# Second weight gather, two memsets and the first angle table rearranged in a spectral layer with a gated FFN

## The chip, the cores and the metric

The kernel runs on one core of a Trainium2 chip. The metric is device time in microseconds of one execution. Five engines work from queues of their own, in order: PE (matrix multiply), DVE (vector), ACT (scalar, activations), POOL (GpSimd) and SP (issues DMAs). They wait for each other through semaphores.

## The reference

The reference is a layer in two halves: a two-dimensional Fourier filter over the normalised input, added to the input, and a gated feed-forward block over the normalised result.

```python
def _A_ref(x, w_r, w_i):          # x: 1 x 2048 x 576
    X = rfft2(x.astype(float32), axes=(-2, -1))
    X = X * (w_r + 1j * w_i)      # 2048 x 289
    return irfft2(X, s=(S, D), axes=(-2, -1)).astype(bfloat16)

def _B_ref(x, w_gate, w_up, w_down):   # 576 -> 4608 -> 576
    return (gelu(x @ w_gate) * (x @ w_up)) @ w_down

h  = x + _A_ref(layernorm(x), w_r, w_i)
h2 = h + _B_ref(layernorm(h), w_gate, w_up, w_down)
```

## The kernel before, in words

The 2048 rows are held as 128 partitions by 16 rows (`h` from 0 to 15, 576 wide). The length-2048 transform is split as 16 x 128. The order of work is written out by hand: each engine runs its instructions in the order in which the program issues them, and nothing reorders them.

**Stage 1, row transforms.** For each row `h`, statistics are taken (on DVE with `sd`, L364, or on ACT with `ln_act`, L121), POOL turns them into 1/sigma (`ln_rstd`, L131: an add L133 and a power L134, four rows at a time), DVE normalises the row (L137, writes `xn`), and PE multiplies it by a 16-point table (`row16` L319, `rests` L335). ACT copies the products from PSUM to `Bt` (`evict` L346, `evict4` L352; the last `evict4`, of rows 12 to 15, is DVE's). `fill` (L309) issues matmuls whose results nobody uses, ahead of rows 0 and 8.

**Tables.** Beside this, three tables are made. `F16` is the 16-point table. `DT` (with `DF`, a part of it in other partitions) is the 576-point column table: sines on ACT (L393), mirrored by DVE (`mirror`, L404), copied into `DF` by L454 and L455; POOL sets `DF` and one column of `DT` to zero first (L446, L447). `TF` holds the twiddle angles' sines and cosines for nine column groups: `first` is the first two of them, `rest` the other seven. For `rest`, DVE makes an integer angle (`angle_a` L237), masks it to 2047 (L264), subtracts 1024 (L265), drops the sign (`angle_c`, L224), and ACT takes `sine` (L271) and `cosine` (L274); L277 makes the negative sine. For `first`, POOL makes the angle in float and takes off whole turns (`first_a` L249, L250; `first_b` L255 to L257), DVE drops a sign (L224), ACT takes the sines (L260, L261). SP then turns `TF` into `TI` by a transposing DMA (`turn_tf`, L280), once for `first`, once for `rest`; thirteen small DMAs (L475) that build `DQ` stand between the two in SP's queue.

**Filter weights.** `WR` and `WI` come half by plain DMA, half by a gather of POOL (`gather`, L382, into `wm_r` and `wm_i`), from which SP copies on (L462). POOL halves two columns of each (L468).

**Stage 2, column loop** (L709). For each column group in `order` (1 to 7, then 0), `f2` (L520) multiplies by the column table for groups k and k+8 and `f2_out` (L531) copies the product out of PSUM as `pq`; `f3` (L537, L538) applies the twiddles, its two halves copied by ACT as `g` and `hs` (L559); `sum_of` (L570) and `wmul` (L588 to L609) on DVE form the filtered spectrum `Zt`; `i3` (L628) starts the inverse with `TI`. For the first group, `f2_out` of group k+8 is DVE's, in two halves, and `sum_of` reads the second half straight from PSUM. PSUM has four buffers of two banks, shared by all these products, so that a product waits for the copy of the one four before it.

**Stage 3.** Inverse columns, residual, and the feed-forward block (L941 and L984), which fills the time from 70 us on with matmuls.

The steps that the change touches are issued in this order before: `gather(0)` after the rstd of rows 4 to 7; `first_a` ahead of the rstd of rows 8 to 11; `first_b` between that and the rstd of rows 12 to 15; behind that on POOL `gather(1)` and the two memsets L446, L447, then the `Zt` memsets (L460). On DVE, the sign drop for `first`, the last `evict4`, `angle_a(rest)`, the negative sine of `first`, `angle_b(rest)`, the copies L531 of the second column product (group 9), `angle_c(rest)`. On ACT, the `rest` sine and cosine stand between the first `pq` copy and the first `g`.

Of the kernel before, what the change touches and what calls it, by code (L numbers as in the profile page):

```python
# [9 lines left out]
ACT = mybir.ActivationFunctionType  # L10
ALU = mybir.AluOpType
FP32 = mybir.dt.float32
# [8 lines left out]
P = 128  # L21
S = 2048
# [5 lines left out]
JH = JP // 2  # L28
# [8 lines left out]
PI = 3.1415925  # L37
# [5 lines left out]
def kernel_body(  # L43
# [12 lines left out]
    V = nc.vector  # L56
    A = nc.scalar
    G = nc.gpsimd
# [23 lines left out]
    zerob = const("zerob", 0.0)  # L82
    pib = const("pib", PI)
    npib = const("npib", -PI)
    hpib = const("hpib", 0.5 * PI)
# [19 lines left out]
    DT = keep.tile([P, 3, 2, 2, JH], BF16, name="DT")  # L105
    D3 = DT[:, 2]
    DF = keep.tile([P, 2, 2, JH], BF16, name="DF")
# [13 lines left out]
    def ln_act(h):  # L121
        for i, fn, sc in ((0, ACT.Identity, 1.0 / D), (1, ACT.Square, 1.0 / D**0.5)):
            junk = roll.tile([P, D], BF16, name="junk", tag="junk", bufs=2)
            A.activation(junk[:], h_sb[:, h, :], fn, scale=sc, accum_out=mv[:, h, i : i + 1])  # L124
# [6 lines left out]
    def ln_rstd(dst, src, lo, hi):  # L131
        sl = slice(lo, hi)
        G.tensor_scalar(dst[:, sl], src[:, sl, 1], 1e-5, None, op0=ALU.add)  # L133
        G.tensor_tensor(dst[:, sl], dst[:, sl], mhalf[:, sl], ALU.pow)  # L134
# [27 lines left out]
    TF = sp.tile([P, 9, 3, P], BF16, name="TF")  # L162
# [6 lines left out]
    def tmp(name, shape, dtype=I32):  # L169
        return scr.tile(shape, dtype, name=name)  # L170
# [15 lines left out]
    q16 = tmp("q16", [P, P], FP32)  # L186
# [10 lines left out]
    C23 = 8388608.0  # L197
# [17 lines left out]
    s2p = tmp("s2p", [P, 1], FP32)  # L215
# [4 lines left out]
    ks = tmp("ks", [P, 9], FP32)  # L220
    V.tensor_scalar(ks[:], kv[:], s2p[:, 0:1], 0.125, op0=ALU.mult, op1=ALU.mult)

    def drop_sign(dst, src):
        V.tensor_scalar(  # L224
            dst.bitcast(I32),
            src.bitcast(I32),
            1,
            1,
            op0=ALU.logical_shift_left,
            op1=ALU.logical_shift_right,  # L230
        )

    pr, ab = tmp("pr", [P, 9, P]), tmp("ab", [P, 9, P], FP32)

    def angle_a(sl):
        n = sl.stop - sl.start
        V.scalar_tensor_tensor(  # L237
            pr[:, sl],
            q16[:].unsqueeze(1).to_broadcast([P, n, P]),
            s2p[:, 0:1],  # L240
            ks[:, sl].unsqueeze(2).to_broadcast([P, n, P]),
            op0=ALU.mult,
            op1=ALU.add,
        )

    qs, prf, abf = (tmp(n, [P, w, P], FP32) for n, w in (("qs", 1), ("prf", 2), ("abf", 2)))

    def first_a():
        G.tensor_scalar(qs[:, 0], q16[:], s2p[:, 0:1], None, op0=ALU.mult)  # L249
        G.tensor_tensor(  # L250
            prf[:], qs[:].to_broadcast([P, 2, P]), ks[:, 0:2].unsqueeze(2).to_broadcast([P, 2, P]), ALU.add
        )

    def first_b():
        G.tensor_scalar(abf[:], prf[:], 1.0 / S, C23, op0=ALU.mult, op1=ALU.add)  # L255
        G.tensor_scalar(abf[:], abf[:], -C23, -float(S), op0=ALU.add, op1=ALU.mult)
        G.tensor_tensor(prf[:], prf[:], abf[:], ALU.add)  # L257

    def first_sines():
        A.activation(TF[:, 0:2, 2, :], prf[:], ACT.Sin, bias=zerob[:], scale=2.0 * PI / S)  # L260
        A.activation(TF[:, 0:2, 1, :], abf[:], ACT.Sin, bias=hpib[:], scale=-2.0 * PI / S)  # L261

    def angle_b(sl):
        V.tensor_scalar(pr[:, sl], pr[:, sl], 2047, None, op0=ALU.bitwise_and)  # L264
        V.tensor_scalar(ab[:, sl], pr[:, sl], -1024.0, None, op0=ALU.add)  # L265

    def angle_c(sl):
        drop_sign(ab[:, sl], ab[:, sl])

    def sine(sl):  # L270
        A.activation(TF[:, sl, 2, :], pr[:, sl], ACT.Sin, bias=pib[:], scale=-2.0 * PI / S)  # L271

    def cosine(sl):
        A.activation(TF[:, sl, 1, :], ab[:, sl], ACT.Sin, bias=nhpib[:], scale=2.0 * PI / S)  # L274

    def minus_sine(sl):
        V.tensor_scalar(TF[:, sl, 0, :], TF[:, sl, 2, :], -1.0, None, op0=ALU.mult)  # L277
# [12 lines left out]
    def row_table():  # L290
        V.scalar_tensor_tensor(
            F16[:, 0:2, :],
            iu[:].rearrange("p c l -> p (c l)").unsqueeze(1).to_broadcast([P, 2, P]),
            0.0,
            fs[:].unsqueeze(1).to_broadcast([P, 2, P]),
            op0=ALU.is_equal,
            op1=ALU.mult,
        )
# [2 lines left out]
        V.tensor_scalar(F16[:, 2, :], F16[:, 0, :], -1.0, None, op0=ALU.mult)  # L301

    ps_f = {}
    FILL = {0: 14, 8: 12}

    def fill(dst, n):

# [3 lines left out]
    def row16(h):  # L311
        if h % 2 == 0 or h == H - 1:
            ps_f[h] = two("f2t")
        f2t, b = (ps_f[h], 0) if h in ps_f else (ps_f[h - 1], 1)
        fill(f2t[:, b, :], FILL.get(h, 0))
        x = xn[:, h, :]
# [64 lines left out]
    def gather(i):  # L381
        G.indirect_dma_start(  # L382
            out=wm[i][:],
            out_offset=None,
            in_=(A_w_r, A_w_i)[i].rearrange("(a r) j -> a (r j)", r=8),
            in_offset=bass.IndirectOffsetOnAxis(ap=rev[:, 0:1], axis=0),
        )
# [4 lines left out]
    def col_sin(r, src, bias):  # L392
        A.activation(  # L393
            DT[:, :, :, r, 0:JM],
            src[:].rearrange("p t (a j) -> p t a j", a=2),
            ACT.Sin,
            bias=bias[:],
            scale=-2.0 * PI / D,
        )
# [8 lines left out]
    first, rest = slice(0, 2), slice(2, 9)  # L408
    for h in (1, 3, 5, 7, 9, 11):
        ln_act(h)  # L410
    row_table()
    sd(0, 2)
    minus_row()
# [14 lines left out]
    sd(8)  # L428
    norms(4, 8)
    rests(4)  # L430
    first_a()
    sd(10, 12)
    ln_fin(slice(9, 12, 2))
    ln_rstd(rstd, mv, 8, 12)
    col_sin(1, pd, zerob)
    col_sin(0, kd, hpib)
    evict(4, 6)
    evict4(4)
    sd(13, 14, 15)
    flush()  # L440
    first_b()
    norms(8, 12)
    ln_rstd(rstd, mv, 12, 16)
    rests(8)
    gather(1)
    G.memset(DF[:], 0.0)  # L446
    G.memset(DT[:, :, 1, :, JH - 1], 0.0)  # L447
    norms(12, 16)
    rests(12)
    evict(8, 10)  # L450
# [2 lines left out]
    mirror(0)  # L453
    V.tensor_copy(DF[0:32], D3[0:32])  # L454
    V.tensor_copy(DF[96:128], D3[96:128])  # L455
    drop_sign(abf[:], prf[:])
    evict(12, 14, 15)
    evict4(12)
    for z in Zts:
        G.memset(z[:].rearrange("p a w b j -> p (a w b) j")[:, :, JW:], 0.0)  # L460
    for w, t in ((WR, wm[0]), (WI, wm[1])):
        nc.sync.dma_start(w[:, 9 : H + 1, 0:J], t[:].rearrange("p (r j) -> p r j", r=8))  # L462
    first_sines()
    angle_a(rest)
    minus_sine(first)
    turn_tf(first)
    for w in (WR, WI):
# [21 lines left out]
            )  # L489
    G16v = [G16[:, sign].rearrange("p x q -> p (x q)") for sign in range(2)]  # L490
    A.activation(G16v[0], pt[:, 0, 0 : 2 * P], ACT.Copy, scale=G_SCALE)
    angle_b(rest)

    xn_pool.__exit__(None, None, None)
    spw = tc.tile_pool(name="spw", bufs=1)
# [34 lines left out]
    def f2_out(c, copy=A.copy, rs=slice(0, 2)):  # L530
        copy(  # L531
            pq[c][:, rs].rearrange("p r (j a) -> p r j a", a=2),
            pq_ps[c][:, :, 0:JP].rearrange("p a (r j) -> p r j a", r=2)[:, rs],
        )
# [30 lines left out]
    def sum_of(k, half):  # L565
        g, hs = gk[k], hk[k]
        if half == 0:
            xab[k] = wk.tile([P, 2, 2, JP], BF16, name="xab", tag="xab", bufs=2)
        x = xab[k]
        V.tensor_tensor(  # L570
            x[:, 1, ::-1, 0:J] if half else x[:, 0, :, 0:J],
            g[:, :, 0:J],
            hs[:, :, 0:J],
            ALU.add if half else ALU.subtract,
        )
# [132 lines left out]
    n = len(order)  # L708
    for i in range(n + 1):  # L709
        last = i >= n  # L710
        if not last:
            f2(order[i])
            if i != 1:
                f2_out(order[i])
        if i == 0:
            f2(order[0] + 8)
            for r in range(2):
                f2_out(order[0] + 8, V.tensor_copy, slice(r, r + 1))
            angle_c(rest)
            sine(rest)  # L720
            cosine(rest)
            minus_sine(rest)
            V.tensor_scalar(G16v[1], G16v[0], -1.0, None, op0=ALU.mult)

        if 1 <= i <= n:
            f3(order[i - 1], 0)
            f3(order[i - 1], 1)
            if i == 1:
                f2_out(order[1])
                sum_of(order[0], 0)  # L730
                sum_of(order[0], 1)
            else:
                if i == 2:
                    turn_tf(rest)
                    pre = [load_gu(g) for g in range(3)]
                    nc.sync.dma_start(wd_a[:], wd_view[:, 0:NWA, :])
                wmul(order[i - 2], i - 1, order[i - 1])
        if not last and i:
            f2(order[i] + 8)
            f2_out(order[i] + 8)  # L740
        if last:
            inv_cols(0, 0)
            inv_cols(0, 1)
        if i >= 3:
            for s in range(3):
                i3(order[i - 3], s)
        if last:
            wmul(order[i - 1], i)
        if i == 1:
            scr_pool.__exit__(None, None, None)  # L750
            eop = ctx.enter_context(tc.tile_pool(name="eop", bufs=1, side="right"))
            EO = [eop.tile([P, 5, H, 2, 4, 8], BF16, name=f"EO{x}", tag=f"EO{x}") for x in range(2)]
# [209 lines left out]
    for tcnk in range(4):  # L962
        for gi in range(NG):
# [7 lines left out]
            n = tcnk * NG + gi  # L971
# [91 lines left out]
```

## Time and profile before

| what | value |
|---|---|
| median of 3 runs | 499.56 us (499.13 to 500.4) |
| profiled execution | 498.99 us, span of its instructions 497.2 us |
| granted TensorE clock | 1.0 |
| PE busy | 485.7 us (98%) |
| DVE, ACT, POOL busy | 225.4, 159.4, 31.4 us |
| chain that ended last | PE 93%, DVE 2%, POOL 2%, ACT 1%, DMA 1%, issue 1% |

The span runs from the first to the last instruction. A busy time is a union over the whole span; an engine that is busy for a third of it can still be the one that others wait for in a short stretch. The chain is followed back from the last instruction, at each step to what released it. In the timelines a row is: start in us, length in us, engine, line, operation, what is written and read, how many instructions are merged, and in brackets the idle time before it with what ended it.

### The profile page before, as it was taken

How to read it: one execution, taken by the hardware profiler on the slowest of the kernel's cores; microseconds unless marked ns; L12 is line 12 of the kernel's file. 1: busy time of each engine (PE TensorE's matmuls, PEld its weight loads, DVE VectorE, ACT ScalarE, POOL GpSimd, SP SyncE). 2: the span in 40 equal slices, each digit the busy share in tenths (PEclk: the TensorE clock that was granted, in tenths of full speed). 3: DMA queues.
4: the chain of work that ended last, by engine and by line, in shares of the span. 5: the costliest groups of instructions: out<-in, count | busy, mean ns of one | idle time of the engine just before them, and what ended most of it. 6: DMA issues, size and time to landing. Idle time of an engine off the chain costs nothing.

```text
span 497.2 us, 12763 instructions
## 1 busy us (share of the span) xinstructions
PE 485.7 (98%) x5715; PEld 337.4 (68%) x5715; DVE 225.4 (45%) x448; ACT 159.4 (32%) x284; POOL 31.4 (6%) x82
## 2 busy tenths in 40 slices
PE   6889999999999999999999999999999999999997
PEld 3467789885579965555599855555799655555995
DVE  8999884698632157533311244333221333333111
ACT  8789973322311022232300132323110223233000
POOL 7700010011110001100000000000000000000000
PEclk9999999999999999999999999999999999999999
DMA  8539979949991029988730079987700277770000
GB/s 283 158 86 173 246 145 200 207 101 201 212 213 19 3 68 198 202 157 157 153 73 3 1 167 190 197 157 149 146 3 1 78 156 154 158 150 2 13 15 24
DMA packets 89549, 62.33 MB, mean 125 GB/s; under 512 B 23190, under 2 KB 88086, under 8 KB 89494
## 3 DMA queue, kind: packets, MB, share of 16 engines
q1 hardware_dynamic: 89206, 60.34, 60.2%
q0 software_dynamic: 288, 1.18, 0.8%
q8 instruction: 44, 0.72, 0.6%
q14 instruction: 11, 0.09, 0.1%
HBM read 52.65 MB, written 2.36 MB: 111 GB/s over the span
## 4 chain that ended last, share of the span: by engine, by line
PE 93%; DVE 2%; POOL 2%; ACT 1%; issue 1%; DMA 1%; POOLq 0%; DVEq 0%
PE gu L941 56%; PE acc L984 27%; PE cs_ps L679 2%; PE acc L1003 2%; PE eo_ps L628 2%; PE pq_ps L520 2%; PE y_ps L813 1%; ACT junk L124 1%; PE gh_ps L538 1%; POOL rstd L134 1%; PE gh_ps L537 1%; DVE xn L137 1%; DMA h_sb<-in_A_x_dram 1%; POOL wm_r L382 0%; PE eo_ps L652 0%
## 5 line engine op out<-in xcount | busy, mean ns | idle before, releaser
L941 PE MATMUL gu<-Bt,wgu 64*128 64x512 bf16 (+1 forms) x2646 | 270.6, 363 | 0.0
L941 PEld LDWEIGHTS <-wgu 64*128 64x128 bf16 x2646 | 151.7, 94 | 115.4 <-issue 0.3
L950 DVE TENSOR_TENSOR P_sb<-g_sb,gu 128x512 bf16<-128x512 f32 (+1 forms) x156 | 100.2, 644 | 140.4 <-ACT g_sb L949 140.4
L949 ACT ACTIVATE g_sb<-gu 128x512 f32<-128x512 f32 (+1 forms) x156 | 88.0, 564 | 193.5 <-PE gu L941 192.2
L984 PEld LDWEIGHTS <-P_sb 64*128 64x128 bf16 x2160 | 122.3, 94 | 10.8
L984 PE MATMUL acc<-wd,P_sb 64*128 64x288 bf16 x1440 | 90.9, 283 | 0.0
L993 DVE TENSOR_TENSOR part<-part,acc 128x576 f32<-128x576 f32 x15 | 11.3, 754 | 112.6 <-ACT part L992 112.6
L992 ACT COPY part<-acc 128x576 f32<-128x576 f32 x15 | 9.6, 638 | 122.8 <-PE acc L984 122.8
L984 PE MATMUL acc<-wd_a,P_sb 64*128 64x288 bf16 x720 | 46.8, 283 | 0.0
L520 PE MATMUL pq_ps<-DT,Bt 128*128 128x290 bf16 x64 | 12.3, 286 | 0.7 <-ACT g L559 0.7
L941 PE MATMUL gu<-Bt,wgu_e 64*128 64x256 bf16 (+1 forms) x162 | 12.5, 305 | 0.0
L838 DVE TENSOR_SCALAR hrow<-h_sb,mv,rstd 128x1152 bf16<-128x1152 bf16 x14 | 12.1, 867 | 0.5 <-POOL rstd L876 0.5
L995 DVE TENSOR_TENSOR h_sb<-h_sb,part 128x576 bf16<-128x576 bf16 x15 | 11.4, 758 | 0.5
L520 PEld LDWEIGHTS <-Bt 128*128 128x128 bf16 x96 | 9.2, 97 | 3.4 <-issue 0.9
L134 POOL TENSOR_TENSOR rstd<-rstd,mhalf 128x1 f32<-128x1 f32 (+1 forms) x16 | 11.4, 713 | 1.3
L319 PE MATMUL f2t<-F,xn 128*128 128x256 bf16 x64 | 8.1, 273 | 3.2 <-DVE xn L137 3.1
L941 PEld LDWEIGHTS <-wgu_e 64*128 64x128 bf16 x162 | 10.4, 94 | 1.2
L133 POOL TENSOR_SCALAR rstd<-mv 128x1 f32<-128x1 f32 (+1 forms) x16 | 3.8, 237 | 116.3 <-DVE mv L119 116.0
L309 PE MATMUL f2t<-h_sb,ident 128*128 128x512 bf16 x26 | 7.4, 445 | 3.7 <-DMA h_sb<-in_A_x_dram 3.7
L679 PE MATMUL cs_ps<-DQ,EO 58*128 58x290 bf16 x144 | 10.8, 283 | 0.0
L531 ACT CAST pq<-pq_ps 128x580 bf16<-128x580 f32 x15 | 9.8, 664 | 0.2
L319 PEld LDWEIGHTS <-xn 128*128 128x128 bf16 x64 | 5.8, 98 | 5.8 <-DVE xn L137 4.9
(151 smaller groups left out, 283.3 us busy)
## 6 DMA issues: line engine op xcount, KB each, us to landing
wgu<-in_B_w_gate_dram SPq DMA_DIRECT2D x46, 432.0 KB
wgu<-in_B_w_up_dram SPq DMA_DIRECT2D x46, 432.0 KB
wd_a<-in_B_w_down_dram SPq DMA_DIRECT2D x1, 1728.0 KB
wd<-in_B_w_down_dram SPq DMA_DIRECT2D x1, 1728.0 KB
wd<-in_B_w_down_dram SPq DMA_DIRECT2D x6, 288.0 KB
out_dram<-h_sb SPq DMA_DIRECT2D x3, 576.0 KB
h_sb<-in_A_x_dram SPq DMA_DIRECT2D x4, 288.0 KB
h_sb<-in_A_x_dram SPq DMA_DIRECT2D x2, 576.0 KB
```

Source lines behind the costliest of these rows:

```text
L134: G.tensor_tensor(dst[:, sl], dst[:, sl], mhalf[:, sl], ALU.pow)
L319: T.matmul(f2t[:, b, t * 2 * P : (t + 1) * 2 * P], lhsT=x[:, d0 : d0 + P], rhs=F16[:, n : n + 2, :], start=(n == 0), stop=(n == 1),)
L520: T.matmul(ps[:, par, 0:JP], lhsT=Bt[:, t, col], rhs=DT[:, t // 2, par] if t < 4 else DF[:, par], start=(t == par), stop=(t == 4),)
L628: T.matmul(pv[:, n], lhsT=z[:, a, w].rearrange("p b j -> p (b j)"), rhs=TI[:, ts[k], 1 - a : 3 - a, :], start=(a == 0), stop=(a == 1),)
L679: T.matmul(ps[:, e, 0:JP], lhsT=EO[x][rows, w, 2 * g : 2 * g + 2].rearrange("p h e k l -> p (h e k l)"), rhs=DQ[rows, w] if w or e else DT ...
L838: V.tensor_scalar(hrow[:], h_sb[:, h, :].rearrange("p (r k) -> p r k", k=64).unsqueeze(2).to_broadcast([P, NR, 2, 64]), mv2[:, h, 0:1], rs ...
L941: T.matmul(gu[:, c, 0:n], lhsT=w[rows, r, i * P : (i + 1) * P], rhs=hl[tcnk % 2][rows, r, lo:hi], start=(r == 0), stop=(r == NR - 1),)
L949: A.activation(g_sb, gu[:, 0, 0:n], ACT.Gelu_apprx_tanh)
L950: V.tensor_tensor(p_sb(f)[:, lo:hi], g_sb, gu[:, 1, 0:n], ALU.mult)
L984: T.matmul(accs[i][:, c, 0:DH], lhsT=p_sb(f)[rows, st * P : (st + 1) * P], rhs=wd[f // NWA][rows, f % NWA, c * DH : (c + 1) * DH], start=( ...
L993: V.tensor_tensor(part, part, accs[1][:, :, 0:DH], ALU.add)
L995: V.tensor_tensor(hv, hv, part, ALU.add)
```

## The change

`gather(1)` is issued directly behind the rows 4 to 7 products and ahead of the rstd of rows 8 to 11; the memsets of `DF` and of a `DT` column are issued ahead of the row table, before POOL's first rstd work. The first angles are made as integers by two POOL instructions (angle only, one per group, behind the rstd of rows 8 to 11), and masked, shifted and sign-dropped by DVE after the last `evict4`, with ACT's `sine` and `cosine` in place of the two float forms. The late angles (`rest`) all move behind the DVE copies of the second column product: `angle_a` and `angle_b` at once, `sine` behind the second `pq` copy of ACT, and the other steps (now `angle_s` and `angle_c`) behind the first group's `sum_of`, with `cosine` after the following `f2_out`. `fill` ahead of row 0 has 16 matmuls, not 14.

```diff
-    qs, prf, abf = (tmp(n, [P, w, P], FP32) for n, w in (("qs", 1), ("prf", 2), ("abf", 2)))
     def first_a():
-        G.tensor_scalar(qs[:, 0], q16[:], s2p[:, 0:1], None, op0=ALU.mult)
-        G.tensor_tensor(
-            prf[:], qs[:].to_broadcast([P, 2, P]), ks[:, 0:2].unsqueeze(2).to_broadcast([P, 2, P]), ALU.add
-        )
-    def first_b():
-        G.tensor_scalar(abf[:], prf[:], 1.0 / S, C23, op0=ALU.mult, op1=ALU.add)
-        G.tensor_scalar(abf[:], abf[:], -C23, -float(S), op0=ALU.add, op1=ALU.mult)
-        G.tensor_tensor(prf[:], prf[:], abf[:], ALU.add)
-    def first_sines():
-        A.activation(TF[:, 0:2, 2, :], prf[:], ACT.Sin, bias=zerob[:], scale=2.0 * PI / S)
-        A.activation(TF[:, 0:2, 1, :], abf[:], ACT.Sin, bias=hpib[:], scale=-2.0 * PI / S)
+        for k in range(2):
+            G.tensor_scalar(pr[:, k], q16[:], s2p[:, 0:1], ks[:, k : k + 1], op0=ALU.mult, op1=ALU.add)
     def angle_b(sl):
         V.tensor_scalar(pr[:, sl], pr[:, sl], 2047, None, op0=ALU.bitwise_and)
+    def angle_s(sl):
         V.tensor_scalar(ab[:, sl], pr[:, sl], -1024.0, None, op0=ALU.add)
...
-    FILL = {0: 14, 8: 12}
+    FILL = {0: 16, 8: 12}
...
         ln_act(h)
+    G.memset(DF[:], 0.0)
+    G.memset(DT[:, :, 1, :, JH - 1], 0.0)
     row_table()
...
     rests(4)
-    first_a()
+    gather(1)
     sd(10, 12)
     ln_fin(slice(9, 12, 2))
     ln_rstd(rstd, mv, 8, 12)
+    first_a()
...
-    first_b()
     norms(8, 12)
     ln_rstd(rstd, mv, 12, 16)
     rests(8)
-    gather(1)
-    G.memset(DF[:], 0.0)
-    G.memset(DT[:, :, 1, :, JH - 1], 0.0)
     norms(12, 16)
...
-    drop_sign(abf[:], prf[:])
     evict(12, 14, 15)
     evict4(12)
...
-    first_sines()
-    angle_a(rest)
+    angle_b(first)
+    angle_s(first)
+    angle_c(first)
+    sine(first)
+    cosine(first)
     minus_sine(first)
     turn_tf(first)
...
-    angle_b(rest)
...
                 f2_out(order[0] + 8, V.tensor_copy, slice(r, r + 1))
-            angle_c(rest)
-            sine(rest)
-            cosine(rest)
-            minus_sine(rest)
-            V.tensor_scalar(G16v[1], G16v[0], -1.0, None, op0=ALU.mult)
+            angle_a(rest)
+            angle_b(rest)
...
             if i == 1:
                 f2_out(order[1])
+                sine(rest)
                 sum_of(order[0], 0)
                 sum_of(order[0], 1)
+                angle_s(rest)
+                angle_c(rest)
+                minus_sine(rest)
+                V.tensor_scalar(G16v[1], G16v[0], -1.0, None, op0=ALU.mult)
...
             f2_out(order[i] + 8)
+            if i == 1:
+                cosine(rest)
```

## The prediction

> **What bounds the kernel now.** The chain on the page gives PE 93% of the span, and the busy strip shows PE at 9 from the third slice on. Read in order of time, the chain is PE without a break from 31.42 us to the end; only the first 31 us belong to others. The change touches only what is issued before about 36 us, so its worth is how much earlier PE's unbroken run begins, no more. First view: the chain in order of time (start, length, what).
>
> ```profile
> 18.36 1.05 POOL rstd L134
> ...
> 19.43 3.16 DVE xn L137 x4
> 22.59 0.81 DVE DT L404 x4
> ...
> 28.71 1.04 ACT TF L274
> 29.75 0.53 ACT g L559
> 30.28 1.09 ACT pq L531 x2
> ...
> 31.42 0.28 PE gh_ps L538
> ```
>
> Four normalisations take 3.16 us here; the same four take 1.64 us at 11.24. Second view: DVE's timeline, cut to two of the normalisations of rows 8 to 15, and POOL's beside it.
>
> ```profile
> 17.29 0.83 DVE L137 TENSOR_SCALAR xn<-h_sb,mv,rstd 128x576 bf16<-128x576 bf16 x1
> ```
>
> ```profile
> 19.84 2.08 DVE L137 TENSOR_SCALAR xn<-h_sb,mv,rstd 128x576 bf16<-128x576 bf16 x1
> ```
>
> ```profile
> 17.09 0.87 POOL L257 TENSOR_TENSOR prf<-prf,abf 128x256 f32<-128x256 f32 x1
> ...
> 19.58 1.12 POOL L382 DMA_INDIRECT wm_i<-in_A_w_i_dram,rev  x1 [0.18 <-issue]
> 20.71 0.59 POOL L446 MEMSET DF<- 128x580 bf16 x1
> 21.23 0.14 POOL L447 MEMSET DT<- 128x6 bf16 x1
> 21.27 0.48 POOL L460 MEMSET Zt<- 128x120 bf16 x3
> 21.84 0.54 POOL L468 TENSOR_SCALAR WR<-WR 128x34 bf16<-128x34 bf16 x1
> ```
>
> A normalisation alone takes 0.42 us. Row 9's took 0.83 and ended 0.16 after L257 did; row 13's took 2.08 and ended only when the gather and five memsets had passed. That is 1.66 us lost to POOL's train. Third view: ACT's timeline, because ACT must copy out what those rows yield.
>
> ```profile
> 18.83 1.93 ACT L346 CAST Bt<-f2t 128x1024 bf16<-128x1024 f32 x2 [1.39 <-PE f2t L319]
> 20.64 0.60 ACT L352 CAST Bt<-f 128x512 bf16<-128x512 f32 x1
> 22.62 1.99 ACT L346 CAST Bt<-f2t 128x1024 bf16<-128x1024 f32 x3 [1.37 <-PE f2t L319]
> ...
> 28.71 1.04 ACT L274 ACTIVATE TF<-ab,nhpib 128x896 bf16<-128x896 f32 x1 [0.89 <-DVE ab L224]
> ...
> 32.52 0.65 ACT L559 CAST hs<-gh_ps 128x578 bf16<-128x578 f32 x1
> ```
>
> ACT idles 1.37 us for row 13 before 22.62. Its copy hs of the second column pair ends at 33.17; DVE's sum for that pair starts at 33.20 and DVE then works without a gap in rounds of 3.57 us (L588 at 35.43, 39.00, 42.58, 46.15), PE in rounds of 3.56. So **the end of that hs copy sets the pace of the loop**: the forecast is its new time.
>
> **Part 1, POOL's second gather and memsets.** They leave the rows 12 to 15. The gather now stands behind the first, which ends at 12.79: with the idle 0.2 and 1.12 to 1.37 (the two gathers' rows) it ends at 14.1 to 14.4, where POOL stood at 14.13 before. Beside it DVE runs statistics, not normalisations. Its transfer now meets the end of the first WI load and the first gather's (landed at 14.1 and 16.15), and SP can issue the WI copy some 6 us earlier; nobody needs WI before about 31, so a slow landing costs nothing by itself. Then sq, mv, rstd, pow as before (14.13 to 16.04, 1.91): 16.0 to 16.3, needed by DVE at 17.00. Then the two new angle products, 0.4 each by L199's rows (two operations, 128x146, 0.38 to 0.40) or 0.63 by L249's: 16.9 to 17.6. I take 0.45, near L199, which has the same two operations. The last rstd pair (18.05 to 19.40, 1.35) then ends at 18.5 to 19.0, and rows 8 to 11 occupy DVE until about 18.8, so row 12 starts near 18.9 and not 19.43. The Zt memsets (0.48) and the WR product (0.54) still fall beside rows 13 and 14 and may hold DVE up to 1.1 us: all four are done at 20.3 to 21.5. ACT is the later one. Its copies for rows 8 to 15 follow at 0.91, 0.90, 0.51, 0.91, 0.48 and 0.60 (starts in the trace, 18.83 to 21.15 and 22.62 to 24.61): 18.83 + 4.31 = 23.14, not 24.61. **1.47 us gained**, and rows 13 and 15 are in time if done by 20.4 and 21.8.
>
> Here one rule of the Trainium skill speaks against the change. SBUF — State Buffer, section "Who interferes with whom", says that of a GpSimd instruction and a DVE one in a two-port mode the first issued has the shared port pair for its whole length while the other blocks. Row 9 behind L257 agrees (0.83 us); rows 5 to 7 beside the first gather do not (1.30 us for three). By the rule the later angle product, if it ends at 17.6, holds row 8 and moves ACT's start by 0.3 us; the sum would then gain 0.3 and not 0.6.
>
> **Part 2, what is late next.** PE's first column product starts 0.11 after ACT's last copy (24.61 to 24.72); twelve matmuls end 1.66 after that (24.72 to 26.38). DVE's copies of the second product then start at 23.14 + 0.11 + 1.66 + 0.05 = 24.96; at 27.32 before, since the late angles stood ahead of them. Behind these copies DVE now runs: copies 0.74, angle_a 1.17, the mask 0.53, two sums 1.36, minus 1024 0.66, sign drop 0.65 (spacings of L531, L237, L264, L570, L265, L224), 5.11 together. ACT's late cosine can start at 30.07, where it started at 28.71. Behind it in ACT's queue are the third pq copy, g and hs of the second pair: 0.95 + 0.54 + 0.54 + 0.65 = 2.68. The hs copy ends at 32.75, not 33.17: **0.42 us**, the other 1.05 of the 1.47 having gone back to the longer chain through the late angles. DVE reaches its sum at about 31.9 and waits for ACT.
>
> The first angles do not lie on that path: sine and cosine wait for three DVE steps (0.29 each by L224 on 128x256, 0.03 between) behind the last L352 copy, about 22.95, so the cosine ends near 24.4, then G 0.3 and the first pq copy, ended near 25.2; PE needs it with the second product's copy at 25.4. If DVE is held there, it costs one for one beyond 0.2.
>
> **Part 3, SP's queue.** The first table transpose (L280) starts at 26.28, behind L277 on DVE; it can now start near 24.5. Thirteen DQ issues and the second transpose follow without a gap (27.73 to 41.01), so the latter ends 1.8 us earlier. In the round at 43.01 PE's weight load began 0.33 after Zt was written (42.65), against 0.10 and 0.15 in the rounds before: I put the other **0.2 us** down to that transpose, and count it back.
>
> **Parts at nothing.** Two more fill matmuls (0.22 each, L309) go into PE's idle 0.72 before 9.05. DF and DT memsets (0.59, 0.14) at 5.9 stand before a POOL step that waited for ACT until 6.59; the pow then ends near 8.4 instead of 8.24, and DVE needs it at 8.57. If that cover fails, 0.3 at most. POOL loses 2.9 us of float angle work (L249 to L257), and DVE swaps one sign drop (0.29) for three steps of that size, counted above.
>
> **Sum.** 0.42 + 0.2 = 0.6 us. The profiled execution took 498.99 (span 497.2 and 1.79 around it): 498.4. The median, 499.56, is 0.57 above it, so the forecast in its terms is 499.56 - 0.6 = **499.0**. That is 0.12%; this kernel's measurement can tell about 0.3%, 1.5 us.
>
> **Rivals.** *The gain goes through.* If the loop were paced by DVE's first product (new start 30.5, was 31.83), 1.3 us would stay, with the 0.2 about 1.5: 498.1, and 0.4 less if row 9 isn't held at 17.29 any more. For it: DVE's rounds are its longest work. Against: hs stands behind the cosine in one queue. *POOL collides later.* The WI product and the m memsets (28.06 to 29.14, 1.04 + 0.34 + 0.32) now fall at 21.5 to 23, since the gather lands 4.6 us after its issue and the WI copy 3.85 after its own: amid DVE's mirrors, copies and first angles. At the most 1.7 us are held there: 499.0 + 1.7 = 500.7, about half likely, 499.8: slower than before once 0.6 us are held. Against: those memsets are small, and some of DVE's time there is a wait for PE. *The gather holds POOL.* Two gathers back to back have no row; if the second waited for the first to land (4.7 us after 11.42) before its 1.12, POOL would end its pow at 19.2 to 19.6 and DVE would start row 8 2.2 to 2.6 us late: 501.4. It decides once the second takes over 0.7 us more than its row. Against: POOL went on 0.06 after the first.
>
> **How the numbers follow.** Forecast 0.70, gain through 0.12, POOL collides 0.12, gather holds POOL 0.06. Faster by over 0.3%: the second with a little of the first, 0.13. Slower: the last and the far end of the third, 0.09. Within: 0.78. The range, 498.1 to 500.4, takes in the held row, the unheld one and most of the collisions, and leaves out the far gains and the waiting gather.
>
> **What would show it.** Row 13's normalisation near 0.4 to 1.1 us; ACT's copies without a gap from 18.8 to 23.2; the second gather within 1.5 us of the first's end; DVE's L531 pair near 25.0; the late cosine near 30.1 with ACT idle before it; hs of the second pair ending near 32.75; no extra wait in the third round. Wrong if ACT's copies show gaps at 21 to 23, if the cosine starts before 29.3 or after 30.8, or if PE's run from 36 us on has new holes.

## The result, and the profile after

| what | before | after |
|---|---|---|
| median of 16 runs each | 499.12 us (498.64 to 500.4) | 498.11 us (497.94 to 498.53) |
| profiled execution, its span | 498.99, 497.21 | 498.27, 496.49 |
| row 8's normalisation starts | 17.00 | 17.31 |
| last `Bt` copy of ACT ends | 24.61 | 23.14 |
| `hs` copy of the second pair ends | 33.17 | 32.66 |
| second table transpose lands | 42.87 | 41.13 |
| third inverse round starts on PE | 43.01 | 42.29 |

The ratio is 0.998, with a 95% interval of 0.9973 to 0.9988: 0.6 to 1.35 us faster, a difference that is real and smaller than 0.3%. The two profiled executions differ by 0.72 us, and so do the starts of their third inverse rounds: from there on PE runs the same work without a new hole. The third inverse round is `i3` of the third column group, the first that reads what the second table transpose wrote. The four steps to that round follow, each in the profile of after. Most lines of the code shown here are 11 lower than before, since functions became shorter (L548 is the old L559, L520 the old L531; L137, L134 and L224 stay).

The chain in order of time (start, length, what):

```profile
29.34 0.64 DVE ab L224
...
30.00 1.04 ACT TF L263
31.04 0.53 ACT pq L520
31.57 0.55 ACT g L548
32.12 0.54 ACT hs L548
...
33.25 0.28 PE gh_ps L527
```

The chain no longer passes through POOL's power step. It runs through the late sign drop on DVE, the late cosine and the three copies queued behind it on ACT, as the prediction's Part 2 had it. DVE's timeline shows the same from the other side:

```profile
17.31 1.40 DVE L137 TENSOR_SCALAR xn<-h_sb,mv,rstd 128x576 bf16<-128x576 bf16 x4
18.96 1.57 DVE L137 TENSOR_SCALAR xn<-h_sb,mv,rstd 128x576 bf16<-128x576 bf16 x4 [0.25 <-POOL rstd L134]
...
24.89 0.83 DVE L520 CAST pq<-pq_ps 128x290 bf16<-128x290 f32 x2 [0.77 <-PE pq_ps L509]
...
32.69 0.47 DVE L559 TENSOR_TENSOR xab<-g,hs 128x578 bf16<-128x578 bf16 x1 [0.92 <-ACT hs L548]
```

Rows 12 to 15 take 1.57 us together; the longest, row 12 beside the `Zt` memsets, takes 0.55, the other three 0.41 to 0.42. The copies of the second product come at 24.89, and the sum of the second pair waits 0.92 us for ACT. POOL's timeline:

```profile
12.71 0.96 POOL L371 DMA_INDIRECT wm_i<-in_A_w_i_dram,rev  x1 [0.30 <-ACT Bt L335]
...
16.02 0.88 POOL L248 TENSOR_SCALAR pr<-q,s2p,ks 128x128 int32<-128x128 f32 x2
...
17.86 1.06 POOL L134 TENSOR_TENSOR rstd<-rstd,mhalf 128x4 f32<-128x4 f32 x1
18.88 0.46 POOL L447 MEMSET Zt<- 128x120 bf16 x3
...
23.95 0.41 POOL L458 TENSOR_SCALAR WI<-WI 128x34 bf16<-128x34 bf16 x1 [2.92 <-DVE ab L224]
```

The second gather follows the first and takes 0.96 us; an angle product takes 0.44; the last power step ends at 18.92. That step, 1.06 us long, lies beside rows 9 to 11 and holds none of them (four rows in 1.40). ACT's timeline:

```profile
18.83 1.93 ACT L335 CAST Bt<-f2t 128x1024 bf16<-128x1024 f32 x2 [1.34 <-PE f2t L308]
20.64 0.60 ACT L341 CAST Bt<-f 128x512 bf16<-128x512 f32 x1
21.12 2.02 ACT L335 CAST Bt<-f2t 128x1024 bf16<-128x1024 f32 x3
```

The copies run without a gap and end at 23.14, where the profile before had 1.37 us of idle for row 13.

### The profile page after: what moved, and what is told of

It reads as the page before. It is cut to its first block, busy times and chain, and to the rows that moved or that the text cites. A ratio compares the mean times of both kernels' runs of the same rounds, so it can differ in the third digit from the quotient of the medians.

```text
span 496.5 us, 12765 instructions
## 1 busy us (share of the span) xinstructions
PE 486.4 (98%) x5717; PEld 339.7 (68%) x5717; DVE 224.0 (45%) x450; ACT 159.3 (32%) x284; POOL 28.5 (6%) x79
## 4 chain that ended last, share of the span: by engine, by line
PE 95%; DVE 3%; DMA 1%; ACT 1%; SPq 0%; issue 0%
PE gu L934 56%; PE acc L977 27%; PE cs_ps L668 2%; PE pq_ps L509 2%; PE acc L996 2%; PE eo_ps L617 2%; DMA h_sb<-in_A_x_dram 1%; PE y_ps L806 1%; PE f2t L308 1%; PE gh_ps L527 1%; PE gh_ps L526 1%; DVE xn L137 1%; DVE st L358 1%; DVE st L360 0%; DVE xab L559 0%; SPq L75 0%
## 5 line engine op out<-in xcount | busy, mean ns | idle before, releaser
L298 PE MATMUL f2t<-h_sb,ident 128*128 128x512 bf16 x28 | 8.7, 478 | 3.7 <-DMA h_sb<-in_A_x_dram 3.7
L134 POOL TENSOR_TENSOR rstd<-rstd,mhalf 128x1 f32<-128x1 f32 (+1 forms) x16 | 11.3, 705 | 1.3
L520 ACT CAST pq<-pq_ps 128x580 bf16<-128x580 f32 x15 | 9.8, 663 | 0.0
L527 PE MATMUL gh_ps<-pq,TF 128*128 128x289 bf16 x32 | 8.2, 286 | 1.5 <-ACT pq L520 1.5
L668 PEld LDWEIGHTS <-EO 58*128 58x128 bf16 x160 | 7.8, 94 | 2.4 <-issue 0.7
```

Source lines behind the costliest of these rows:

```text
L527: T.matmul(dst, lhsT=TF[:, ts[k1], t1, :], rhs=b, start=False, stop=True)
L668: T.matmul(ps[:, e, 0:JP], lhsT=EO[x][rows, w, 2 * g : 2 * g + 2].rearrange("p h e k l -> p (h e k l)"), rhs=DQ[rows, w] if w or e else DT ...
```

## The experiments

The first theory was the prediction's: POOL's gather and memsets held rows 12 to 15 and moving them gains the 1.47 us on ACT, while the late angles give most of it back. The rivals were that the memsets alone did the holding, and that the gain came from the angle part, which lets POOL deliver the last 1/sigma earlier. Runs e1, e2, e4, e5 and e12 take the change apart; e10 and e8 test the places of the late angles and of the transpose; e3, e6, e7, e9 and e11 move what the chain then showed.

| run | ratio to before (95%) | span | `hs` ends | transpose lands | third round |
|---|---|---|---|---|---|
| before | 1 | 497.21 | 33.17 | 42.87 | 43.01 |
| after | 0.998 (0.9973 to 0.9988) | 496.49 | 32.66 | 41.13 | 42.29 |
| e4, angles alone | 0.9993 (0.9984 to 1.0002) | 496.91 | 32.79 | 42.57 | 42.71 |
| e5, both moves alone | 0.9988 (0.9979 to 0.9997) | 496.91 | 32.90 | 42.58 | 42.71 |
| e12, memsets alone | 0.999 (0.9981 to 1.0) | 496.73 | 32.14 | 42.39 | 42.53 |
| e3, cosine later | 0.996 (0.9947 to 0.9974) | 495.41 | 30.73 | 41.07 | 41.21 |

In all of these the span changes by what the third round changes by, to 0.01 us. In the first five kernels DVE has written the third `Zt` 9.49 to 9.50 us after the `hs` copy ends, and the third round starts 0.13 to 0.14 us after the later of two events: that `Zt`, or the landing of the second table transpose (the last completion that the trace records for it). Before, e4, e5 and e12 start that long after the landing; after starts 0.14 after `Zt` (42.15). So **two paths meet there**, and the change as a whole moved both: `hs` by 0.51 and the landing by 1.74. The timelines show the last steps, first those of before, then those of after:

```profile
37.66 3.35 SPq L280 DMA_TRANSPOSE TI<-TF  x1
...
42.20 0.45 DVE L609 TENSOR_TENSOR Zt<-zb,za 128x580 bf16<-128x580 bf16 x1
...
43.01 0.49 PE L628 MATMUL eo_ps<-TI,Zt 128*128 128x256 bf16 x3
```

```profile
35.83 3.90 SPq L269 DMA_TRANSPOSE TI<-TF  x1
...
41.70 0.46 DVE L598 TENSOR_TENSOR Zt<-zb,za 128x580 bf16<-128x580 bf16 x1
...
42.29 1.25 PE L617 MATMUL eo_ps<-TI,Zt 128*128 128x256 bf16 x10
```

Row 8's start moves between executions by itself: after, e3, e6, e7 and e10 have the same code up to it, and it lies at 17.31, 17.20, 16.86, 17.19 and 17.05; in e4 and e8, which are alike up to it, at 17.36 and 17.02. Where two kernels are compared below "from the same start", this difference is taken off the span; that is an estimate.

**e1, the gather put back** behind the last rstd:

```diff
     rests(4)
-    gather(1)
...
     rests(8)
+    gather(1)
```

> The changed kernel with the second gather alone put back behind the rstd of rows 12 to 15 (memsets stay early). My theory, that POOL's whole train held row 13: the gather runs about 19.1 to 20.2, row 13's normalisation is held again and ends at 20.5 to 21.0 instead of 19.84, ACT's copy of row 12 starts up to 0.5 us later than 21.12, and the time is 0 to 0.5 us over the changed kernel. Rival, that the large memset alone held row 13: row 13 takes 0.4 to 0.55 us and the time is that of the changed kernel within 0.2 us. Second rival, that the gather alone held it: row 13 takes over 1.2 us.

Measured: 498.3 us, ratio 0.9983 (0.9974 to 0.9992), span 496.48, as after. DVE's timeline:

```profile
18.94 1.54 DVE L137 TENSOR_SCALAR xn<-h_sb,mv,rstd 128x576 bf16<-128x576 bf16 x4 [0.25 <-POOL rstd L134]
```

Four rows in 1.54 us, with the gather on POOL from 19.09 to 20.33: it held none of rows 12 to 14 (0.42 to 0.43 us each; row 15, which ran on past the gather's end, took 0.52). My theory's hold did not appear; the rival's numbers did. The late gather did cost the other path: the second transpose landed at 41.69 and not at 41.13, which cost nothing here because `Zt` came later still, at 42.13.

**e2, the memsets put back**:

```diff
-    G.memset(DF[:], 0.0)
-    G.memset(DT[:, :, 1, :, JH - 1], 0.0)
     row_table()
...
     rests(8)
+    G.memset(DF[:], 0.0)
+    G.memset(DT[:, :, 1, :, JH - 1], 0.0)
```

> The changed kernel with the two memsets of DF and DT alone put back behind the rstd of rows 12 to 15 (gather stays early). Theory of the train: memsets from 18.9 to 20.0 with those of Zt hold row 12 or 13 until they are over, one normalisation takes 0.9 to 1.5 us; ACT's copy of row 12 starts at 21.12 to 21.4, time 0 to 0.3 us over the changed kernel. Rival, that the gather alone held row 13: no normalisation over 0.6 us.

Measured: 498.35 us, ratio 0.9982 (0.9973 to 0.9991), span 496.30. POOL's timeline:

```profile
18.58 0.57 POOL L434 MEMSET DF<- 128x580 bf16 x1
...
19.14 0.46 POOL L447 MEMSET Zt<- 128x120 bf16 x3
```

Row 12 started at 18.66 and took 1.11 us, until 19.77; the last memset ends at 19.60. The memsets do hold a normalisation, for longer than the first of them lasts: five stand in a row there. The Trainium skill, page SBUF — State Buffer, section "Who interferes with whom", has the shared port pair as a lock for the length of an instruction; that row 12 waits agrees, and the unheld rows beside the power step and beside the gather of e1 do not. The hold cost little time here, because ACT was still busy with older rows: its copy of row 12 started 0.57 us behind the one before it (20.34 to 20.91), where after has 0.48.

**e4, the angle part alone** (gather, memsets and 14 fills as before):

```diff
-    FILL = {0: 16, 8: 12}
+    FILL = {0: 14, 8: 12}
...
-    G.memset(DF[:], 0.0)
-    G.memset(DT[:, :, 1, :, JH - 1], 0.0)
     row_table()
...
     rests(4)
-    gather(1)
...
     rests(8)
+    gather(1)
+    G.memset(DF[:], 0.0)
+    G.memset(DT[:, :, 1, :, JH - 1], 0.0)
```

> The angle part of the change alone: gather, memsets and fill stay as in the kernel before. My theory: POOL reaches the gather 0.5 us earlier, row 13 is held as before until about 21.1, ACT's last copy ends near 24.1 (24.61 before), but the way from there to the hs copy of the second pair is 9.6 us and not 8.56, so hs ends at 33.6 to 33.8 (33.17 before): 0.2 to 0.6 us slower than the kernel before, the earlier transpose giving 0.2 back. Rival, that the angle part brings the gain: 0.5 us or more faster than the kernel before.

Measured: 498.69 us, ratio 0.9993 (0.9984 to 1.0002), span 496.91: 0.3 us below before, not above it. DVE's timeline:

```profile
19.01 2.31 DVE L137 TENSOR_SCALAR xn<-h_sb,mv,rstd 128x576 bf16<-128x576 bf16 x4 [0.25 <-POOL rstd L134]
```

Rows 14 and 15 were held (0.94 and 0.76 us), but rows 12 and 13 were done at 19.78, beside the gather (from 19.16) and ahead of the memsets (from 20.42), since the last 1/sigma came at 18.97 and not at 19.40. ACT's copies ran without a gap from 18.88, and the last ended at 23.20: **1.41 of the 1.47 us come without any of the moves**. From that copy to the end of `hs` it took 9.59 us (expected 9.6). What was lost was the other path. SP's timeline:

```profile
25.14 2.04 SPq L269 DMA_TRANSPOSE TI<-TF  x1
...
37.23 3.31 SPq L269 DMA_TRANSPOSE TI<-TF  x1
```

The late gather's copy into `WI` stands ahead of the first transpose in SP's queue (24.43), the transpose took 2.04 us where it took 1.33 in after, and the second landed at 42.57. That longer issue is 0.71 of the 1.40 us by which the second transpose was issued later than in after. Another 0.65 are the later start of the first (25.14 for 24.49): it stood behind ACT's first cosine (ended at 25.10), and ACT had waited 0.80 us for DVE, which came late from the held rows 14 and 15. The third round started 0.42 us past `Zt` (42.29 to 42.71), 0.14 behind the landing.

**e5, both moves alone** (before, with gather and memsets moved, float angles kept):

```diff
+    G.memset(DF[:], 0.0)
+    G.memset(DT[:, :, 1, :, JH - 1], 0.0)
     row_table()
...
     rests(4)
+    gather(1)
     first_a()
...
     rests(8)
-    gather(1)
-    G.memset(DF[:], 0.0)
-    G.memset(DT[:, :, 1, :, JH - 1], 0.0)
```

> The moves alone: gather and memsets moved as in the change, all angles as in the kernel before (float angles on POOL, late angles ahead of the second column copy). My theory: POOL does its float angles before the rstd of rows 12 to 15, which is ready near 20.2 instead of 18.9; row 13 ends near 21.0, ACT's copy of row 12 starts near 21.7 (22.62 before, 21.12 changed), its last copy ends near 23.7, and the way from there to the hs copy stays 8.56: hs near 32.3, so 0.8 to 1.1 us faster than the kernel before, as fast as the changed kernel within 0.4 us. Rival, that the change needs both parts: within 0.3 us of the kernel before.

Measured: 498.63 us, ratio 0.9988 (0.9979 to 0.9997), span 496.91, 0.3 us better and not 0.8 to 1.1. DVE's timeline:

```profile
17.51 2.25 DVE L137 TENSOR_SCALAR xn<-h_sb,mv,rstd 128x576 bf16<-128x576 bf16 x4 [0.45 <-POOL rstd L134]
20.73 1.56 DVE L137 TENSOR_SCALAR xn<-h_sb,mv,rstd 128x576 bf16<-128x576 bf16 x4 [0.96 <-POOL rstd L134]
```

The gather, now ahead of POOL's float angles, pushed everything behind it: DVE waited 0.45 and 0.96 us for 1/sigma, rows 8 to 10 were held beside the float angles (0.62, 0.56 and 0.89 us), and the last copy ended at 24.41. From there to the end of `hs` it was 8.49 us, as before (8.56). The early gather needs the lighter angle part.

**e12, the memsets alone** (before, with the two memsets early):

```diff
+    G.memset(DF[:], 0.0)
+    G.memset(DT[:, :, 1, :, JH - 1], 0.0)
     row_table()
...
     gather(1)
-    G.memset(DF[:], 0.0)
-    G.memset(DT[:, :, 1, :, JH - 1], 0.0)
```

> The kernel before with nothing changed but the two memsets of DF and DT, issued early as in the change (gather, float angles, late angles and fill stay). The theory that is left after the first runs, that a memset of POOL and not the gather held row 13: row 13 takes 0.42 to 0.6 us instead of 2.08, ACT's copy of row 12 starts near 21.2 instead of 22.62, the way from its last copy to the hs copy stays 8.5, hs ends at 31.1 to 31.6 instead of 33.17, and the time is 1.4 to 2.0 us under the kernel before, so 0.4 to 1.0 us under the whole change. Rival, that the gather holds it: row 13 over 1 us, under 0.6 us gained.

Measured: 498.51 us, ratio 0.999 (0.9981 to 1.0), span 496.73: 0.48 us, a third of what was expected. Row 13 took 0.96 us (19.88 to 20.85) where before it took 2.08; ACT's last copy ended at 23.62, 0.99 earlier, and `hs` at 32.14, 1.03 earlier. Two moved memsets did more for `hs` than the whole change. ACT's copies ran without a gap here too; their end is not the full 1.47 earlier only because the first started at 19.31 and not at 18.83, row 8 having started at 17.36 and been held beside POOL's float angles (0.81 us). The wait view of the third round, and POOL's timeline, say why so little of it remained and what still held row 13:

```profile
PE eo_ps L628 <- DMA TI<-TF: 0.6, 1, 0.6
```

```profile
19.62 1.12 POOL L382 DMA_INDIRECT wm_i<-in_A_w_i_dram,rev  x1 [0.18 <-issue]
```

`Zt` was there at 41.63, the transpose landed at 42.39. Row 13 ended 0.11 after the gather did (20.74): here a gather held one for about 0.5 us. That cost nothing, since ACT's copy of row 12 stood behind older ones until 21.60.

**e10, the late angles in their old place** (after, with `angle_a` behind the first transpose, `angle_b` and `angle_s` behind the `DQ` loads, the rest behind the second product's copies):

```diff
     turn_tf(first)
+    angle_a(rest)
...
+    angle_b(rest)
+    angle_s(rest)
...
-            angle_a(rest)
-            angle_b(rest)
+            angle_c(rest)
+            sine(rest)
+            cosine(rest)
+            minus_sine(rest)
+            V.tensor_scalar(G16v[1], G16v[0], -1.0, None, op0=ALU.mult)
...
```

> The changed kernel with the late angles put back where they were: angle product, mask and minus 1024 ahead of DVE's copies of the second column product, sine and cosine behind ACT's first pq copy. My theory, that the way from ACT's last copy to the hs copy grew from 8.56 to 9.5 us by the new place of the late angles: second-product copies start near 26.4 instead of 24.89, but the late cosine starts near 27.8 instead of 30.00 and hs of the second pair ends near 32.1 to 32.3 instead of 32.66: 0.3 to 0.6 us faster than the changed kernel. Rival, that the earlier copies are what pays: as slow as the kernel before, or 0.5 us and more slower than the changed kernel.

Measured: 497.77 us, ratio 0.9973 (0.9963 to 0.9984), span 495.85, 0.64 below after; 0.26 of that is row 8, which started at 17.05 in place of 17.31. The cosine starts at 27.55 and not at 30.00, and `hs` ends 9.13 us after ACT's last copy, where after has 9.52. So copying the second product ahead of the late angles costs about 0.4 us.

**e8, the angle part with half the `DQ` loads behind the transpose** (e4, and the six loads of `r == 0` issued after the second `turn_tf`):

```diff
-    for r in (1, 0):
+    def load_dq(r):
...
+    load_dq(1)
...
                     turn_tf(rest)
+                    load_dq(0)
```

> The angle part alone (gather, memsets, fill as before) with the later half of SP's DQ issues moved behind the second table transpose, so that this lands some 4 us earlier. Its parent, the angle part alone, had its hs copy end at 32.79, 0.13 us behind the changed kernel's, and a gap of 0.42 us ahead of the third inverse round; span 496.9 against 496.5. My theory, that gather and memsets cost what they cost through the transpose: the gap falls to 0.14, the span to 496.6, within 0.2 us of the changed kernel. Rival, that they cost through DVE or ACT: the span stays at 496.9.

Measured: 498.3 us, ratio 0.999 (0.9981 to 0.9999), span 496.20, third round at 42.00, 0.14 behind `Zt`. Row 8 started at 17.02 here; from the same start, e8 and after both stand at 496.18 (496.20 - 0.02, 496.49 - 0.31). So, by this estimate, beside the new angles the two moves are worth what they give the transpose, and six shifted loads give the same. The medians (498.3 and 498.11, with overlapping intervals) do not contradict it, but are too coarse to show it.

**e3, the cosine later**, behind `g` and `hs` of the second pair on ACT:

```diff
                 if i == 2:
+                    cosine(rest)
                     turn_tf(rest)
...
-            if i == 1:
-                cosine(rest)
```

> The changed kernel with ACT's late cosine moved behind the hs copy of the second pair. My theory, that this copy sets the pace of the loop and stood behind the cosine: hs ends near 30.8 instead of 32.66, DVE's sum for the second pair follows its first products without a wait at 31.7 instead of 32.69, and every later round is 0.9 to 1.0 us earlier: 0.7 to 1.1 us faster than the changed kernel. Rival, that something else paces the loop (the column products, or DVE's later work): under 0.3 us.

Measured: 497.33 us, ratio 0.996 (0.9947 to 0.9974), span 495.41, 1.08 below after, of which 0.11 are row 8's earlier start (17.20). ACT's and DVE's timelines:

```profile
30.08 0.65 ACT L548 CAST hs<-gh_ps 128x578 bf16<-128x578 f32 x1
30.61 1.05 ACT L263 ACTIVATE TF<-ab,nhpib 128x896 bf16<-128x896 f32 x1
```

```profile
31.58 0.46 DVE L559 TENSOR_TENSOR xab<-g,hs 128x578 bf16<-128x578 bf16 x1
```

`hs` ends 1.93 us earlier; the sum starts 1.11 earlier, without a wait, right behind DVE's products. DVE is the bound of the second pair now. So in after the cosine's place in ACT's queue, and not DVE's work, set the pace. The other path is used up as well: `Zt` was there at 41.02 and the transpose landed at 41.07, so the landing, by 0.05 us, sets the third round here.

**e7, the late angle steps ahead of the first sums** on DVE:

```diff
                 sine(rest)
-                sum_of(order[0], 0)
-                sum_of(order[0], 1)
                 angle_s(rest)
                 angle_c(rest)
+                sum_of(order[0], 0)
+                sum_of(order[0], 1)
```

> The changed kernel with DVE's two late angle steps (minus 1024, sign drop) issued ahead of the first group's two sums instead of behind them. My theory: the late cosine starts at 28.8 to 29.0 instead of 30.00, hs of the second pair ends near 31.5 instead of 32.66, DVE's first products start where they did (30.34) and its sum follows at 31.7: 0.7 to 1.0 us faster than the changed kernel. Rival, that the sums in their old place pace the loop (PE's second half waits for them to free PSUM): no faster, or slower by up to the 1.3 us by which they are later.

Measured: 497.26 us, ratio 0.9959 (0.9945 to 0.9972), span 495.48. The cosine starts at 28.82, `hs` ends at 31.48, the sum starts at 31.70. The wait can be taken away from either end.

**e6, the second transpose behind two groups of weight loads** on SP, which asks how late it may come:

```diff
                 if i == 2:
+                    pre = [load_gu(g) for g in range(2)]
                     turn_tf(rest)
-                    pre = [load_gu(g) for g in range(3)]
+                    pre.append(load_gu(2))
```

> The changed kernel with SP's second table transpose behind the first two groups of weight loads (four issues of 0.7 us), so 2.8 us later. My theory, that this transpose's landing gates the third inverse round: it lands near 44.0 instead of 41.13, PE's third round starts near 44.2 instead of 42.29, and the time is 1.5 to 2.2 us over the changed kernel. Rival, that it has slack: no change within 0.3 us.

Measured: 507.88 us, ratio 1.0171 (1.0154 to 1.0189), span 506.1, +9.6 and not the 1.5 to 2.2 expected. SP's timeline, the waits of PE, and three stretches (us; then busy time and count of PE, PEld, DVE, ACT, POOL; granted clock; DMA share; GB/s):

```profile
39.24 8.09 SPq L269 DMA_TRANSPOSE TI<-TF  x1
```

```profile
PE eo_ps L617 <- DMA TI<-TF: 7.5, 1, 7.5
```

```profile
42.00:46.00 4.00, 0.00 (x0) 0.00 (x0) 4.00 (x10) 0.82 (x2) 0.00 (x0) 0.76 1.15 199
46.00:50.00 4.00, 0.46 (x3) 0.37 (x4) 0.62 (x1) 0.00 (x0) 0.00 (x0) 0.50 1.12 207
50.00:54.00 4.00, 4.00 (x19) 2.60 (x18) 0.00 (x0) 1.92 (x3) 0.00 (x0) 0.50 1.12 222
```

Behind the loads the transpose took 8.09 us to issue (3.90 in after) and landed at 49.40. The third round started at 49.54, 7.25 late. The other 2.4 us come after it: the granted clock fell to 0.50 in PE's idle stretch, and its matmuls took 0.45 us and not 0.28 until 54.28. PE was idle from 42.00; narrower stretches of the same view give a clock of 1.00 up to 44.00, 0.61 from 44.00 to 44.50 and 0.50 from there, so the clock fell about 2.1 us into the idle stretch. The Trainium skill, page TensorE: Matmul & The Clock Gate, section "What's actually happening", gives a halved clock after an idle window of about 3.4 us and full speed again after about as much sustained work. The halving agrees; the times differ, and the measured ones count here: 2.1 us on the way down and 4.7 us (49.54 to 54.28) on the way back.

**e9 and e11, the best of these together.** e9 is e3 with `angle_a(rest)` ahead of the second product's copies, the negative sine between the products and the sums of the first `wmul`, and the negative `G` table and the transpose's issue behind that whole `wmul`; e11 adds e8's late `DQ` loads.

```diff
     turn_tf(first)
+    angle_a(rest)
...
         times(WI, m2, slice(0, J))
+        if k == order[0]:
+            minus_sine(rest)
...
-            angle_a(rest)
...
-                minus_sine(rest)
-                V.tensor_scalar(G16v[1], G16v[0], -1.0, None, op0=ALU.mult)
...
+                wmul(order[i - 2], i - 1, order[i - 1])
+                if i == 2:
+                    V.tensor_scalar(G16v[1], G16v[0], -1.0, None, op0=ALU.mult)
...
```

> The late cosine behind the hs copy of the second pair, and DVE's road to its first filter product shortened: the late angle product goes ahead of the copies of the second column product, where DVE waited 0.76 us for PE; the late negative sine goes between the first filter products and the sum; the negative 16-point table goes behind the first round. With the cosine moved alone, hs ended at 30.73 and DVE was what came late (first product 30.23, sum 31.58). My theory: first product at 29.5 to 29.7, sum of the second pair at 31.2 to 31.4, span 495.0 to 495.3 (495.4 with the cosine moved alone), and a gap of 0.1 to 0.3 ahead of the third round, as the transpose now lands too late. Rival, that DVE's road isn't what is late after that: 495.4 or more.

> The version with the late cosine behind hs and DVE's road shortened (span 495.3, with a gap of 0.55 us ahead of the third inverse round), with the later half of the DQ issues behind the second table transpose. My theory, that this gap was the transpose's landing: the gap falls to 0.15 and the span to 494.9 to 495.0. Rival: the gap stays, or the next wait takes its place, and the span stays at 495.3.

Measured, e9: 497.04 us, ratio 0.9956 (0.9942 to 0.9969), span 495.33; DVE's sum starts at 31.00, `Zt` is there at 40.58, and the transpose at 41.00 is the later one again. e11: 496.91 us, ratio 0.9957 (0.9943 to 0.997), span 495.38 with row 8 0.35 us later than in e9; the transpose landed at 38.76, far ahead, and the third round began 0.24 behind `Zt` (40.94) where e9 had 0.55. From the same start e11 would be 0.30 ahead, but the medians do not tell the two apart. Both lie below after, their intervals clear of its own.

## Why the prediction was right, and where it was wrong

**The bound.** Held: `hs` of the second pair was forecast to end at 32.75 and ended at 32.66, with ACT idle for 0.96 us before the late cosine (forecast 30.07, measured 30.00). But it was only one of two bounds: before, the third round began 0.14 behind the transpose, with `Zt` written 0.21 ahead of it, so an earlier `hs` by itself would have saved nothing. The prediction had those 0.21 as its 0.2 of Part 3 and summed the two, which is right as long as the landing moves by at least 0.21 more than `hs` does (it moved by 1.74, and the bound went from the landing at 42.87 to `Zt` at 42.15: 0.72, or 0.21 + 0.51). In e12, 1.03 us on `hs` end as 0.48 because the landing moved by only that.

**Part 1.** The number held (23.14 forecast, 23.14 measured; the last power step at 18.92 in the forecast 18.5 to 19.0; the gather took 0.96, its end 13.67 ahead of the forecast 14.1). The reason did not hold: the 1.47 us were put down to the gather and memsets leaving rows 12 to 15. e4 closes ACT's gap with both still there (copies from 18.88 to 23.20), and e12 closes it with two memsets moved (19.31 to 23.62). Either is enough, they do not add, and with the float angles kept both moves together end the last copy only 0.20 earlier (e5).

**The term that was too small.** Row 9 was forecast to be no longer held only in a rival ("0.4 less"); in the forecast's sum it stood at nothing, as ACT's start was kept at 18.83. In after row 9 takes 0.42, and ACT starts at 18.83 only because row 8 came 0.31 us later, its statistics having waited for the input's DMA. In e2 and e8, where row 8 starts at 17.01 and 17.02, ACT starts at 18.53 and 18.54: 0.30 earlier than before from the same start. That 23.14 was met exactly is therefore luck: the unheld row 9 and the later row 8 cancel. With the term the forecast 0.6 would have been 0.9. That the medians show 1.0 and the profiles 0.72 for this reason is worked out, not shown: the start of row 8 is known only in the profiled executions.

**Part 2.** 0.42 was forecast for `hs`, 0.51 measured; 1.05 us given back, 0.96 measured (9.52 against 8.56 from the last copy to `hs`). e10 puts 0.39 of that on the late angles' new place; the other 0.57 stays with the new angle part as a whole and was not divided.

**Part 3.** The gap of the third round is gone, as forecast; the first transpose was issued at 24.49 (forecast: near 24.5) for 26.28, and the second 1.83 us earlier (35.83 for 37.66). It takes both parts of the change: the landing is earlier by 0.30 with the angles alone (e4), by 0.29 with the moves alone (e5), and by 1.74 with both.

**The base.** The forecast 499.0 started from the median 499.56 of three runs; the median of 16 is 499.12. Of the 0.89 us by which the result lies lower, 0.44 are that; the row-9 term accounts for 0.30 of the other 0.45.

**The rivals.** *The gain goes through*: its place was wrong, since DVE's product started at 30.34 and DVE then waited for `hs`. That its 498.1 lies beside the measured 498.11 is luck: it was 1.5 us under a base that stood 0.44 too high, and 1.0 was measured. *POOL collides later*: no. `WI` arrived late, one packet at 23.88 when the others were there by 22.33, and its product (23.95) and the `m` memsets (24.23) fell beside the end of DVE's first negative sine (23.90, 0.23 us) and into its wait for PE ahead of 24.89. *The gather holds POOL*: no, 0.96 us. By the rule of the Trainium skill that the prediction gives (SBUF — State Buffer, "Who interferes with whom") the later angle product might have held row 8; the second ended at 16.90, ahead of row 8, so no run here shows that case. **Parts at nothing** held: the early memsets (5.86, 6.38) left the power step ending at 8.42, ahead of 8.57. In after row 0 itself came only at 9.29, but in e3, which has the same early memsets and 16 fill matmuls, it came at 8.45 and PE's first row product 0.48 us later, as before (8.57 to 9.05). The two more fill matmuls were not tried by themselves; e8, with 14, stands where after does by the estimate above.

**Open.** When a gather holds a normalisation: about 0.5 us in e12 (row 13), and in e4 row 14, 0.94 us long, began 0.54 us into the gather and ended 0.23 after it; in e1 row 14 began 0.54 us into the gather too and took 0.42. POOL's spans are rough, and no run was made that shifts only that overlap.

## What to carry to other kernels

Where two paths meet at one instruction, find the arrival time of each before costing an edit: the gain is what the later of the two moves (0.48 of the 1.03 us on `hs` in e12, where the transpose came 0.48 earlier), and moving the later one alone yields at most the slack between them. In an engine's in-order queue, look at what a waiting instruction stands ahead of: the late cosine cost about 1.0 us by standing ahead of the copies that pace the loop, though the same work fitted behind them (e3). And when two edits both remove a hold, take the parts singly before giving either the credit.

## What was not expected of the hardware

A transposing DMA behind four weight loads on the same queue took 8.09 us to issue and landed 10.16 us after its issue began (39.24 to 49.40); ahead of them 3.90 and 5.30 (35.83 to 41.13). The first transpose took 1.75 to 2.04 us where the copy into `WI` was issued within 1.2 us ahead of it (e1, e4, e8, e12), and 1.33 in after. An idle PE of 7.5 us cost 2.4 us more afterwards, while the granted clock was 0.50 for the 4.7 us behind it.
